# Attention with sigmoids and a token mixer on one core: the order of the work, three transposed head groups, double sigmoids and held loads

## The chip, the cores and the metric

The program runs on one core of a Trainium2 chip. Its engines are PE (TensorE, matrix products into PSUM), ACT (ScalarE), DVE (VectorE), POOL (GpSimd) and SP, which issues the DMAs. Each engine works through its own queue in order; semaphores make one wait for another. The metric is the device time of one execution in microseconds (us), as a median of several.

## The reference

For 8 batches and 12 heads, with sequences of 448 and head size 64, float32:

```python
scores = scale * np.matmul(q, k.transpose(0, 1, 3, 2)) - np.log(S)
attn = 1.0 / (1.0 + np.exp(-scores))
attn_out = np.matmul(attn, v)
x = attn_out.transpose(0, 2, 1, 3).reshape(B, S, H * D)
wq, wk = x @ w_q, x @ w_k
W_tok = scale * np.einsum('bsd,btd->bst', wq, wk)
mixed = np.einsum('bst,btd->bsd', W_tok, x)
out = np.maximum(mixed, 0.0) @ w_out
```

## The kernel before

Four heads of one batch make a group; there are 24 groups, three to a batch, counted from 0. Each group is cut into 7 tiles of 64 keys, so there are 168 tiles of scores, counted here from 1: tiles 1 to 7 belong to group 0, tile 8 is the first of group 1.

For each group q, k and v are loaded in float32 and cast to bf16, mostly by POOL. q and k are then transposed, in one of three ways, by the group's letter in the plan: on PE against an identity matrix and copied out of PSUM ("q", "k"); or by DVE in 32 x 32 blocks, from a layout that POOL has arranged ("c", "d") or in parts by DVE alone ("r", "s", "z"). On PE, `transposes` takes 28 products of 64 x 64 for one array, four of them side by side; `transposes_whole` takes 7 of 128 x 128 and has been used for group 0 alone. Groups 1 to 3 and 6 go by PE; of group 1 each array is copied out by itself (L280), of the others q and k together in one copy (L288).

`scores` makes one tile: four products of 64 x 448 into one pair of PSUM banks, and one sigmoid on ACT (L305) that writes an `at` tile, one of 16. `values` (L311) multiplies `at` with v and adds up over the seven tiles of a group; the result xt is copied out (L328) and transposed for the mixer (`tr_x`). When the three groups of a batch are done, the mixer follows: wq and wk (`mlp_wqk`), a transposition (`mlp_wkn`), `mlp_tmp`, `mlp_mix`, and the output projection in half-chunks of six or twelve products (`out_chunk`, `out_pair`), each copied out (L584, L530) and stored by SP.

PSUM is one array of eight banks, handed out as four pairs, 0 to 3, or as single banks a to h (a and b make pair 0, and so on to g and h in pair 3). Which one each step takes stands in the string BANKS.

The order is written out by hand: PLAN is a string of letters, and the loop at its end (L762) issues one step for each, onto the engines' queues. S makes a tile of scores, P a value product (its case says, where it is the last of a group, which engine copies out), q, k, c, d, r, s, z transpose, W, N, U, M are the mixer's steps, O and o half-chunks of the output with the copy by DVE or ACT, D lets one store be issued, E is four products of zeros whose result nobody uses, K the transposition of the last four parts of group 0's k, 1 a cast by DVE. Loads follow a list, ORDER, into a ring of six buffers (`pump_loads`, L658): a load is issued when the buffer's last content has been cast. Entries with a dot are cast by DVE.

The kernel has a mechanism by which a load waits for a matmul (`behind_product`, L174): places would be marked by "^" in ORDER and "G" in PLAN. Neither occurs, so no load waits in that way.

Of the kernel before, what the change touches and what calls it, by code (L numbers as in the profile page):

```python
# [10 lines left out]
BF16 = mybir.dt.bfloat16  # L11
U32 = mybir.dt.uint32
ACTF = mybir.ActivationFunctionType
# [4 lines left out]
def kernel(  # L18
# [12 lines left out]
    nc = tc.nc  # L31
    B, H, S, HD = q.shape
# [3 lines left out]
    P = 128  # L36
    NI, NP = 7, 64
# [18 lines left out]
    p_x = pool("x", 2)  # L56
    p_one = pool("one", 1)
    p_mx = pool("mx", 2)
# [4 lines left out]
    banks = ps_q.tile([P, 8, 512], F32, tag="banks", name="banks")  # L63
# [1 line left out]
    pairs = [banks[:, 2 * n : 2 * n + 2] for n in range(4)]  # L65
    pairs16 = [banks16[:, 2 * n : 2 * n + 2] for n in range(4)]
    BANKS = (
        "abcd01230100233111102130123012312123120c302302023d0231a30123"
        "01310321312302103210e13f01fe30123c20312032a32b3213023ab12313"
        "2b13231023a213023a2b13ab213a21302gh012g012012303e013210ef130"  # L70
        "fe1302302g102h120h120321gh201gh201g12302a123ba123013ab12312g"
        "h102312gh1023132132032013031201231231031a2102302132103103123"
        "13103213023a1203203102"
    )
    given = list("".join(BANKS))
    held = set()
# [41 lines left out]
    products = []  # L118
# [11 lines left out]
    def xt(u, j):  # L130
        return xts[u % 2 * NJ + j].rearrange("p i h n -> p h i n")


    TW = (2, 3,)


    PLAN = (
        "KSSESDDESD1SEDqEE1EDSSkpPppSDppPSSSqDS1kpSPDpSqSpSkSpPSPSxSx"
        "wrDSSDDSwwspSpPppSzPPSSrwSwWXSsPSPpSpPNPPSUSqSzMSSkSPPPDDSSp"
        "DMppDSPSxSDxMScSpPpPSSdPpSDPWwwSSWDrXwWSSOsONSPpPSppzpSPSOOS"  # L140
        "xSPrpPpSUpSPszPSOSOSoSoSppMSPPPPPSSwcWWOCwSSdxOwSMWSOSxOSDMp"
        "DPScpDppSPDPSOdDoSDpxPPSCPPrSDPPDSOOSNSsSOzoOOSUSXcSDPpdpSSP"
        "pPSPOOwSMSWoWwMSSOWWScCpPpSxpdpSpPSOOMrSPPpSPpSSPPOoNSSSDszo"
        "oDOoDpxDSPpDpxSppPDSuWcdwWSSMWOOSMSWwOOSDxppSPcPSpmpPDooDNSD"
        "SSdooooDSSxODOSUPSDpPDpDSpPDPOcDOSSSOoodOSpMPSppPSPPcSwWwoSM"
        "SdOwWSSWOONSPMpcpSPpSPPSdOoXSoSxoSOxSOpPSpcUPSppPSoOSdSxoOSP"
        "PPmppSPPoSoMcSoSOlmlLLSLLSdooDSODNyOpScpdppPSSPPOoSoSOSOOSUS"
        "oSOpSPpP1SPoSoPSPoSOxpPPmPpPpMllmllyllyooONoOUoommooMOOOOOOO"
        "ooooooOOooOo"
    )  # L150
    PLAN = "".join(PLAN)
    KIND = ["a"] + [t for t in PLAN if t in "qcr"]

    ld = {}
    SRC = dict(q=q, k=k, v=v)
# [70 lines left out]
    qk = {}  # L226
# [28 lines left out]
    def tr(n, nm, kind):  # L255
        t = "qk".index(nm)
        if kind == "s":
            return
        if kind == "r":
            qk[n] = p_qk.tile([P, 2, 2, NI, NP], BF16, tag="qk", name="qk")  # L260
            w = pq[n].rearrange("p e t i d y -> p e (t i d y)").bitcast(F32)
            for e in range(2):
                nc.vector.transpose(out=qk[n][:, e].rearrange("p t i n -> p (t i n)").bitcast(F32), in_=w[:, e])  # L263
            return
        if kind in "cd":
            assert n in arranged
            w = pq[n].rearrange("p e t i d y -> p e (t i d y)").bitcast(F32)[:, t]
            if t == 0:
                qk[n] = p_qk.tile([P, 2, 2, NI, NP], BF16, tag="qk", name="qk")
            nc.vector.transpose(out=qk[n][:, t].rearrange("p t i n -> p (t i n)").bitcast(F32), in_=w)  # L270
            return
        t16 = ld.pop((nm + "16", n))
        if t == 0:
            ps_qk[n] = bank2()
        fb, _, ps = ps_qk[n]
        transposes(ps[:, :, t * S : (t + 1) * S], t16, slice(0, NI))
        if n == 1:
            if t == 0:
                qk[n] = p_qk.tile([P, 2, 2, NI, NP], BF16, tag="qk", name="qk")
            nc.vector.tensor_copy(  # L280
                out=qk[n][:, :, t].rearrange("p h i n -> p h (i n)"), in_=ps[:, :, t * S : (t + 1) * S],
            )
# [12 lines left out]

    def scores(n, i):
        fb, sc, _ = bank2()
        for g in range(2):
            for h in range(2):
                mm(  # L300
                    sc[HALF[h], g, 0:S], qk[n][HALF[g], h, 1, i, :],
                    qk[n][HALF[g], h, 0].rearrange("p i n -> p (i n)"), start=True, stop=True,
                )
        at = p_at.tile([P, 2, S], BF16, tag="at", name="at")
        nc.scalar.activation(at, sc[:, :, 0:S], ACTF.Sigmoid, bias=attn_bias, scale=attn_scale)  # L305
        release(fb)
        ats[n, i] = at

    pv = {}

# [168 lines left out]
    chunks = []  # L479
    ot = {}  # L480

    opened = []
    stores, o_tiles = [], [0]
# [133 lines left out]
    def cols(r):  # L617
# [9 lines left out]
        out=ident, in_=ident, compare_op=ALU.not_equal, fill=1.0, base=0,  # L627
# [4 lines left out]
    for _ in range(32):  # L632
        mm(pairs[3][:, 0, 0:P], zeros[:, 0:P], zeros[:, 0:P], start=True, stop=True)


    ORDER = (
# [5 lines left out]
    )  # L642
    BY = {"s": [], "v": []}
    GATED = {(x.strip(".!^")[0], int(x.strip(".!^")[1:])) for x in ORDER.split() if "^" in x}
    gates = []
    for x in ORDER.replace("^", "").split():
# [5 lines left out]
    ORDER = [(x[0], int(x[1:])) for x in ORDER.replace(".", "").replace("!", "").replace("^", "").split()]  # L652
    done = dict.fromkeys("SPqkKxWNUMOCDz", 0)
    used, loaded, cast = set(), set(), set()

# [2 lines left out]
    def pump_loads():  # L658
        while len(loaded) < len(ORDER):
            nm, n = ORDER[len(loaded)]  # L660
            if len(ring) >= 6 and ring[-6] not in cast:
                break
            if (nm, n) in GATED and not gates:
                break
            m = gates.pop(0) if (nm, n) in GATED else 0
            ring.append((nm, n))
            if nm == "w":
                load_wout(n - 1, m) if n else load_weights()
            else:
                load1(n, nm, nc.sync, m)  # L670
            loaded.add((nm, n))
# [83 lines left out]
    used |= {("q", 0), ("k", 0)}  # L755
    pump()

    ALIKE = dict(c="q", r="q", j="k", d="k", s="k", X="x", y="x", Y="x", z="z", w="W", L="W", l="W")
    done["q"] = done["k"] = 1
    quads_r = []  # L760

    for t in PLAN:  # L762
# [9 lines left out]
        if t in "12":  # L772
            cast_one("vs"[int(t) - 1])
            continue
        if t == "G":
            gates.append(len(products) - 1)
            continue
# [61 lines left out]
    assert not chunks and not opened and not stores and not given and not any(BY.values())  # L839
# [1 line left out]
_INS = ['q', 'k', 'v', 'moe_w_q', 'moe_w_k', 'moe_w_out']  # L841
_OUTS = [((8, 448, 768), 'float32')]
# [25 lines left out]
```

## Time and profile before

| | us |
|---|---|
| median of 3 runs | 186.71 (186.39 to 190.08) |
| the profiled execution, whole | 187.86 |
| its span, first to last instruction | 186.0 |
| mean granted TensorE clock | 0.998 |
| HBM read, written | 35.78 MB, 11.01 MB |

A row of a group names the source line, the engine, the operation, what it writes and reads, the shapes and the count; then the time that the group was busy and the mean of one in ns; then the idle time before it and who ended it. A row of a timeline begins with its start and its length in us. Line L121 is the helper through which all products go, L124 the one for transpositions on PE, so that the tiles' names tell them apart. The end of a product is modelled; the distance of two starts is the safer reading.

### The profile page before, as it was taken

The numbers are of one execution on the slowest core, as the hardware profiler recorded it, in microseconds if no ns is written. First come the engines' busy times: TensorE is split into PE (matmuls) and PEld (weight loads), VectorE is DVE, ScalarE is ACT, GpSimd is POOL, SyncE is SP. The second block draws the span as 40 slices with busy tenths as digits, with TensorE's granted clock in tenths as the row PEclk, the third lists the DMA queues.
The fourth block names the chain that finished last, engine by engine and source line by source line (L and its number), as shares of the span: only waits on it lengthen the run. The fifth ranks groups of instructions, "written<-read, shape, count | busy, mean of one in ns | idle before, by whom it ended". The sixth has DMA issues, their size and how long they took to land.

```text
span 186.0 us, 8450 instructions
## 1 busy us (share of the span) xinstructions
PE 169.6 (91%) x3642; PEld 113.7 (61%) x3642; DVE 134.2 (72%) x206; ACT 158.7 (85%) x205; POOL 116.8 (63%) x156
## 2 busy tenths in 40 slices
PE   7697688789999999999997999999999999999980
PEld 7354435454664555655554556456788798879970
DVE  2545599979998998988985953589786875685430
ACT  4499999999999999999996899899989999966020
POOL 1236697998889996699949969798999300000000
PEclk9999999999999999999999999999999999999999
DMA  5998999979998799999999999995596243333665
GB/s 175 357 380 267 350 343 341 401 247 318 380 392 323 245 273 324 296 273 351 321 234 328 341 289 322 322 338 205 147 321 178 73 110 86 90 88 88 176 169 170
DMA packets 24309, 48.51 MB, mean 261 GB/s; under 512 B 3920, under 2 KB 16464, under 8 KB 24272
## 3 DMA queue, kind: packets, MB, share of 16 engines
q1 hardware_dynamic: 24112, 47.79, 79.6%
q8 instruction: 28, 0.46, 1.0%
q10 hardware_dynamic: 160, 0.20, 0.3%
q14 instruction: 9, 0.07, 0.1%
HBM read 35.78 MB, written 11.01 MB: 252 GB/s over the span
## 4 chain that ended last, share of the span: by engine, by line
PE 70%; DVE 12%; DMA 5%; ACT 4%; issue 3%; POOL 2%; SPq 0%; DVEq 0%; ACTq 0%; POOLq 0%
PE banks L121 67%; PE banks L124 4%; ACT at L305 4%; DVE qk L250 4%; DMA ld<-in_k_dram 2%; DMA ld<-in_moe_w_q_dram 2%; DVE xt L328 2%; DVE xn L357 2%; DVE qk L263 1%; DVE mx L442 1%; POOL wqk L693 1%; POOL qk L210 1%; DVE wqk L402 1%; DVE qk L288 1%; DVE k L220 0%
## 5 line engine op out<-in xcount | busy, mean ns | idle before, releaser
L305 ACT ACTIVATE at<-banks 128x896 bf16<-128x896 f32 x168 | 141.2, 937 | 7.7 <-PE banks L121 6.9
L121 PE MATMUL banks<-wout,mx 64*64 64x384 bf16 (+1 forms) x840 | 65.6, 324 | 0.3 <-issue 0.2
L121 PE MATMUL banks<-qk 64*64 64x448 bf16 x672 | 60.9, 358 | 5.2 <-ACT at L305 2.4
L210 POOL CAST qk<-ld 128x896 bf16<-128x896 f32 x38 | 44.6, 1190 | 9.7 <-issue 6.7
L121 PEld LDWEIGHTS <-mx 64*64 64x64 bf16 (+1 forms) x840 | 39.8, 105 | 16.4 <-issue 6.1
L121 PE MATMUL banks<-at,v 64*64 64x448 bf16 x672 | 47.5, 350 | 0.3 <-ACT at L305 0.2
L121 PEld LDWEIGHTS <-qk 64*64 64x64 bf16 x672 | 27.3, 105 | 25.6 <-issue 18.7
L328 DVE CAST xt<-banks 128x896 bf16<-128x896 f32 x23 | 24.9, 1084 | 9.4 <-PE banks L121 9.1
L121 PEld LDWEIGHTS <-v 64*64 64x64 bf16 x672 | 23.8, 106 | 5.8 <-issue 1.1
L442 DVE TENSOR_SCALAR mx<-banks 128x896 bf16<-128x896 f32 (+1 forms) x21 | 19.9, 955 | 3.9 <-PE banks L121 3.6
L220 POOL CAST v<-ld 128x896 bf16<-128x896 f32 x22 | 20.2, 929 | 2.2 <-DMA ld<-in_v_dram 1.7
L357 DVE COPY xn<-banks 128x896 bf16<-128x896 bf16 x20 | 12.5, 623 | 5.7 <-PE banks L124 4.9
L270 DVE STREAM_TRANSPOSE qk<-qk 128x448 f32<-128x448 f32 x26 | 16.0, 629 | 0.1
L250 DVE STREAM_TRANSPOSE qk<-qk 32x448 f32<-32x448 f32 x24 | 15.3, 636 | 0.6
L169 POOL COPY qk<-qk 32x448 uint32<-32x448 uint32 x26 | 14.4, 554 | 1.6
L172 POOL COPY qk<-swap 32x448 uint32<-32x448 uint32 x26 | 14.4, 554 | 1.5
L121 PE MATMUL banks<-xt,wqk 64*64 64x448 bf16 (+1 forms) x84 | 13.8, 353 | 0.3 <-ACT at L305 0.2
L124 PEld LDWEIGHTS <-xt 64*64 64x64 bf16 (+1 forms) x588 | 9.9, 108 | 2.3 <-DVE xt L328 0.4
L584 DVE COPY o<-banks 128x384 f32<-128x384 f32 x17 | 9.4, 551 | 2.2 <-PE banks L121 1.5
L124 PE MATMUL banks<-ident,xt 64*64 64x64 bf16 (+1 forms) x588 | 10.4, 194 | 0.1
L121 PE MATMUL banks<-wqk,tmp 64*64 64x224 bf16 (+1 forms) x72 | 8.8, 290 | 0.1
L121 PE MATMUL banks<-wq,tmp 64*64 64x224 bf16 (+1 forms) x72 | 8.5, 292 | 0.0
(67 smaller groups left out, 135.6 us busy)
## 6 DMA issues: line engine op xcount, KB each, us to landing
ld<-in_q_dram SPq DMA_DIRECT2D x24, 448.0 KB, 6.3
ld<-in_v_dram SPq DMA_DIRECT2D x24, 448.0 KB, 6.1
ld<-in_k_dram SPq DMA_DIRECT2D x23, 448.0 KB, 6.0
out_dram<-o SPq DMA_DIRECT2D x38, 192.0 KB, 4.4
ld<-in_moe_w_out_dram SPq DMA_DIRECT2D x6, 384.0 KB, 4.9
out_dram<-ld SPq DMA_DIRECT2D x12, 192.0 KB, 2.8
wout<-wout SPq DMA_DIRECT2D x6, 192.0 KB, 7.6
out_dram<-ld SPq DMA_DIRECT2D x6, 96.0 KB, 3.2
```

The lines of the kernel that those rows point to most:

```text
L121: products.append(nc.tensor.matmul(*args, **kw))
L124: products.append(nc.tensor.transpose(*args, **kw))
L169: eng.tensor_copy(out=w[lo, 1], in_=w[hi, 0])
L172: eng.tensor_copy(out=w[hi, 0], in_=z[lo])
L210: COPY[e](out=f[:, :, "qk".index(nm)].rearrange("p e i d y -> p e y i d"), in_=ld.pop((nm, n)).rearrange("p (y i e d) -> p e y i d", y=2, ...
L220: COPY[e](out=t16.rearrange("p i b d -> p b i d"), in_=ld.pop((nm, n)).rearrange("p b (i d) -> p b i d", i=NI),)
L250: nc.vector.transpose(out=qk[n][other : other + 32, h].rearrange("p t i n -> p (t i n)").bitcast(F32), in_=w[own : own + 32, 1 - h],)
L270: nc.vector.transpose(out=qk[n][:, t].rearrange("p t i n -> p (t i n)").bitcast(F32), in_=w)
L305: nc.scalar.activation(at, sc[:, :, 0:S], ACTF.Sigmoid, bias=attn_bias, scale=attn_scale)
L328: COPY[eng](out=xt(u, j), in_=ps)
L357: COPY[eng](out=xn, in_=ps)
L442: nc.vector.tensor_scalar(dst, ps, moe_scale, 0.0, ALU.mult, ALU.max)
```

## The change

Four things change, and the written-out order is a new one.

1. Groups 1, 2 and 3 are transposed by `transposes_whole`: 7 products of 128 x 128 for q and 7 for k, each array into a single bank and copied out by DVE by itself (letters a, b). Group 6 alone is still transposed by 28 products.
2. A step T makes the scores of a tile without a sigmoid; the next S makes another tile, and then one sigmoid covers both, reading two bank pairs in one access with a step between them. The 16 `at` tiles become one array, so that two neighbours can be written at once. T occurs four times: tiles 2 and 3, 6 and 7, 116 and 117, 124 and 125 share a sigmoid.
3. A table BEHIND names 18 loads and, for each, a matmul by its number, behind which the load begins. The older marks are gone.
4. PLAN, BANKS and ORDER are new. There are ten E instead of six; two more xt tiles are transposed whole (Y); the first tile of scores stands ahead of K; w_q and w_k are loaded ahead of group 3 and cast by DVE; D occurs 77 times, not 46.

```diff
-    p_at = pool("at", 16)
+    at_all = singles.tile([P, 16, 2, S], BF16, name="at")
...
-        "KSSESDDESD1SEDqEE1EDSSkpPppSDppPSSSqDS1kpSPDpSqSpSkSpPSPSxSx"
+        "SDKTSDDSEEEESTEES1abEESD1PpPSpppDPSDaSbSDEDPS1PSDPSDPxSESPDD"
...
-        "DPScpDppSPDPSOdDoSDpxPPSCPPrSDPPDSOOSNSsSOzoOOSUSXcSDPpdpSSP"
+        "pPNDDppPPSDSODDOOcSTSOOOoSdxSoXDpDcSdPDDppSPUpDSPSDDOoDTSODD"
...
-    KIND = ["a"] + [t for t in PLAN if t in "qcr"]
+    KIND = ["a"] + [t for t in PLAN if t in "qacr"]
...
         t16 = ld.pop((nm + "16", n))
+        if kind in "ab":
+            fb, _, ps = bank1()
+            transposes_whole(ps, t16, slice(0, NI))
+            if t == 0:
+                qk[n] = p_qk.tile([P, 2, 2, NI, NP], BF16, tag="qk", name="qk")
+            nc.vector.tensor_copy(
+                out=qk[n][:, :, t].rearrange("p h i n -> p i h n"),
+                in_=ps[:, 0 : NI * P].rearrange("p (i h n) -> p i h n", h=2, n=NP),
+            )
+            release(fb)
+            return
...
-    def scores(n, i):
+    begun = []
+
+    def scores(n, i, alone):
...
-        at = p_at.tile([P, 2, S], BF16, tag="at", name="at")
-        nc.scalar.activation(at, sc[:, :, 0:S], ACTF.Sigmoid, bias=attn_bias, scale=attn_scale)
-        release(fb)
-        ats[n, i] = at
+        begun.append((fb, n, i))
+        if not alone:
+            return
+        slot = (NI * begun[0][1] + begun[0][2]) % 16
+        begun.sort()
+        for x, (_, m, c) in enumerate(begun):
+            ats[m, c] = at_all[:, slot + x]
+        if len(begun) == 1:
+            dst, src = at_all[:, slot], sc[:, :, 0:S]
+        else:
+            (lo, _, _), (hi, _, _) = begun
+            dst = at_all[:, slot : slot + 2]
+            src = banks.rearrange("p (a b) x -> p a b x", b=2)[:, lo : hi + 1 : hi - lo, :, 0:S]
+        nc.scalar.activation(dst, src, ACTF.Sigmoid, bias=attn_bias, scale=attn_scale)
+        for f, _, _ in begun:
+            release(f)
+        begun.clear()
...
+    BEHIND = {('v', 3): 216, ('q', 5): 216, ('k', 5): 216, ('k', 6): 216, ('q', 7): 216, ('w', 4): 216, ('v', 5): 472, ('w', 6): 472, ('k', 9): 600, ('q', 11): 856, ('v', 11): 984, ('k', 13): 1112, ('v', 14): 1368, ('v', 16): 1496, ('q', 17): 1496, ('k', 20): 1880, ('v', 22): 2264, ('v', 23): 2392}
...
-            if (nm, n) in GATED and not gates:
+            m = BEHIND.get((nm, n), 0)
+            if m >= len(products):
                 break
-            m = gates.pop(0) if (nm, n) in GATED else 0
...
-        if t == "S":
-            scores(*divmod(c, NI))
+        if kind == "S":
+            scores(*divmod(c, NI), t == "S")
```

What this does to the queues shows in the built programs, row by row in their order. First ACT, from its last copy for group 0 on; `at` are the sigmoids' results. Before:

```order
L740 COPY qk_164<-banks_85 128x3x2x64
L305 ACTIVATE at_206<-banks_85 128x896
L305 ACTIVATE at_212<-banks_85 128x896
L305 ACTIVATE at_222<-banks_85 128x896
L305 ACTIVATE at_232<-banks_85 128x896
L305 ACTIVATE at_244<-banks_85 128x896
```

And now:

```order
L765 COPY qk_162<-banks_82 128x3x2x64
L330 ACTIVATE at_89<-banks_82 128x896
L330 ACTIVATE at_89<-banks_82 128x1792
L330 ACTIVATE at_89<-banks_82 128x896 x2
L330 ACTIVATE at_89<-banks_82 128x1792
L330 ACTIVATE at_89<-banks_82 128x896 x51
L461 CAST tmp_1248<-banks_82 128x384
```

Seven sigmoids have become five, two of them over two tiles, and a copy for the mixer has come in after the 58th tile.

Next PE, at the last scores of group 0 that stand ahead of group 1's transposition (q16_234 before, q16_180 now, is q of group 1; qk_164, qk_162 group 0's transposed q and k; the brackets name the engines waited for). Before:

```order
L121 LDWEIGHTS qk_164
L121 MATMUL banks_85<-qk_164 64x448 [waits Activation_49]
L121 LDWEIGHTS zeros_91
L121 MATMUL banks_85<-zeros_91 64x448 [waits Activation_49]
L124 LDWEIGHTS q16_234 [waits DVE_49]
L124 MATMUL banks_85<-ident16_90,q16_234 64x64
```

And now:

```order
L121 LDWEIGHTS zeros_88
L121 MATMUL banks_82<-zeros_88 64x448
L121 LDWEIGHTS qk_162
L121 MATMUL banks_82<-qk_162 64x448
L124 LDWEIGHTS q16_180 [waits Pool_49]
L124 MATMUL banks_82<-ident16_87,q16_180 128x128 [waits Activation_49]
```

The transposition now stands behind all seven tiles of group 0, not behind some of them, and its first product waits for ACT; the count that it waits for is the one that the second sigmoid over two tiles brings.

Last PE at the scores of tiles 115 to 117 (qk) and the output projection behind them (wout, mx). Before:

```order
L121 MATMUL banks_85<-qk_2542 64x448 [waits Activation_49]
L121 LDWEIGHTS qk_2542
L121 MATMUL banks_85<-qk_2542 64x448
L121 LDWEIGHTS mx_2113
L121 MATMUL banks_85<-wout16_86,mx_2113 128x384 [waits Activation_49]
```

And now:

```order
L121 MATMUL banks_82<-qk_2262 64x448 [waits Activation_49]
L121 LDWEIGHTS qk_2262
L121 MATMUL banks_82<-qk_2262 64x448
L121 LDWEIGHTS mx_1913
L121 MATMUL banks_82<-wout16_83,mx_1913 128x384 [waits Activation_49]
```

The rows read alike. The count behind the last bracket was that of an earlier copy by ACT; it is now that of the sigmoid over tiles 116 and 117, whose scores stand directly ahead.

More of the change, by code (lines that the diff above doesn't have):

```diff
@@ L67 @@
     BANKS = (
[L68 to L73, printed above, removed]
+        "abcd012301222220333cd222103e0f1330210200c21a2310e3101013f013"
+        "2a103103120312030231203123c2032d0c3d20c32320312031e31f301232"
+        "cd30230c230230132c302131ef301efg01203120c230dc230230121g2013"
+        "2a32ba312b3210323ab21321b321a30cd230cd203c203103c02dc302130c"
+        "d3202dc302130cd320131231201201321321021301301201303c21320120"
+        "320310312312012g12a3201203102"
     )
@@ L131, in xt @@
         return xts[u % 2 * NJ + j].rearrange("p i h n -> p h i n")
-    TW = (2, 3,)
+    TW = (2, 3)
     PLAN = (
-        "KSSESDDESD1SEDqEE1EDSSkpPppSDppPSSSqDS1kpSPDpSqSpSkSpPSPSxSx"
-        "wrDSSDDSwwspSpPppSzPPSSrwSwWXSsPSPpSpPNPPSUSqSzMSSkSPPPDDSSp"
-        "DMppDSPSxSDxMScSpPpPSSdPpSDPWwwSSWDrXwWSSOsONSPpPSppzpSPSOOS"
-        "xSPrpPpSUpSPszPSOSOSoSoSppMSPPPPPSSwcWWOCwSSdxOwSMWSOSxOSDMp"
-        "DPScpDppSPDPSOdDoSDpxPPSCPPrSDPPDSOOSNSsSOzoOOSUSXcSDPpdpSSP"
[L143 to L149, printed above, removed]
+        "SDKTSDDSEEEESTEES1abEESD1PpPSpppDPSDaSbSDEDPS1PSDPSDPxSESPDD"
+        "aDSDDpPSbSxSDSwWPrPSPSPspSzPDPwSSDWSrwXWSsSSpDPPNSpPSDzpUSPS"
+        "MSqkSSpPPppSxPSPMSSxSpcPPSMpPSDpPSWDwWSWDdSSwSrDWXSoOSOSsPNS"
+        "pPppSzpPSOCSDxSuSPrCpSppSPsPzooSPSoOSpcPMSppSPpPSOdWwxSDSOwW"
+        "xcSOSMSWwOMSpdPpSPPPDPSDSOOSPDPpSxDpPSPDPSOONSScSdoOXoSOSDDU"
+        "DSPPpSpSpcPCPSdoOSMSwoWSMDSDWwWwOSSPPpcxPpSpdPSOODSMrDpDppsD"
+        "SPPSpOoDSSPDDNzDOoSSxooDUScDpPPSxPPPSPSwwOSMwDoWdSMSowoWSpmp"
+        "pDNDDppPPSDSODDOOcSTSOOOoSdxSoXDpDcSdPDDppSPUpDSPSDDOoDTSODD"
+        "ooOSMPppSpcDppSPSWdOwDMSWwwoSDDSWooNSMPPDSPpppSDcdSPYOOSSoxO"
+        "cSoxSOpSpppSUSppPSOSodxSOSPOSPPpSPcDPPSOmoMSOmOlSdLlllLSoSOO"
+        "DSxpocDpSNppSppPS1oOSOSdDOOSoSSOopDpUPSPPpSPOSDOSoSoPpyPppmp"
+        "PlLMLDLMYLloOxoNOoUoODMomoMOOooOOooOoOOOooOOoO"
     )
     PLAN = "".join(PLAN)
-    KIND = ["a"] + [t for t in PLAN if t in "qcr"]
+    KIND = ["a"] + [t for t in PLAN if t in "qacr"]
     ld = {}
@@ L651 @@
     OTHERS = set(BY["s"] + BY["v"])
-    ORDER = [(x[0], int(x[1:])) for x in ORDER.replace(".", "").replace("!", "").replace("^", "").split()]
+    ORDER = [(x[0], int(x[1:])) for x in ORDER.replace(".", "").replace("!", "").split()]
     done = dict.fromkeys("SPqkKxWNUMOCDz", 0)
@@ L774 @@
             continue
-        if t == "G":
-            gates.append(len(products) - 1)
-            continue
         kind = ALIKE.get(t, t if t in "qkx" else t.upper())
@@ L838 @@
                 out_chunk(t == "o", tail)
-    assert not chunks and not opened and not stores and not given and not any(BY.values())
+    assert not begun and not chunks and not opened and not stores and not given and not any(BY.values())
 _INS = ['q', 'k', 'v', 'moe_w_q', 'moe_w_k', 'moe_w_out']
```

6 lines of the change are left out of this document (2 added, 4 removed), and 10 rows, old and new, of the table ORDER.

## The prediction

> **What bounds the kernel now.** I read the page's head first, then its chain of waits, the busiest group, and the timeline of ACT by itself.
>
> ```profile
> span 186.0 us, 8450 instructions
> PE 169.6 (91%) x3642; PEld 113.7 (61%) x3642; DVE 134.2 (72%) x206; ACT 158.7 (85%) x205; POOL 116.8 (63%) x156
> PE 70%; DVE 12%; DMA 5%; ACT 4%; issue 3%; POOL 2%; SPq 0%; DVEq 0%; ACTq 0%; POOLq 0%
> L305 ACT ACTIVATE at<-banks 128x896 bf16<-128x896 f32 x168 | 141.2, 937 | 7.7 <-PE banks L121 6.9
> ```
>
> PE and ACT are both nearly full, and 70% of the chain is PE. The shares hide two regimes, which ACT's own timeline shows:
>
> ```profile
> 5.12 0.48 ACT L740 COPY qk<-banks 128x384 bf16<-128x384 bf16 x1 [0.57 <-PE banks L124]
> 7.46 13.16 ACT L305 ACTIVATE at<-banks 128x896 bf16<-128x896 f32 x16 [1.86 <-PE banks L121]
> 20.80 39.03 ACT L305 ACTIVATE at<-banks 128x896 bf16<-128x896 f32 x47 [0.18 <-PE banks L121]
> 59.73 0.47 ACT L584 COPY o<-banks 128x384 f32<-128x384 f32 x1
> ```
>
> From 7.46 to 59.8 us ACT runs 63 sigmoids with one gap of 0.18 us. Sixteen take 13.16 us, the last of them 0.94, so one starts every (13.16 - 0.94) / 15 = 0.815 us. This stretch is bound by ACT: whatever delays a sigmoid there delays all later ones, and PE has too little other work to make it up. Later PE leads:
>
> ```profile
> 20.00:30.00 10.00, 8.09 (x160) 4.27 (x160) 8.92 (x13) 9.82 (x13) 8.92 (x11) 1.00 0.99 353
> 110.00:120.00 10.00, 10.00 (x160) 5.62 (x153) 5.32 (x9) 9.16 (x14) 7.86 (x11) 1.00 0.93 318
> PE banks L121 <- ACT at L305: 3.5, 12, 0.5
> PE banks L121 <- DVE xn L357: 1.4, 1, 1.4
> ```
>
> In the rows by windows (PE, PEld, DVE, ACT, POOL busy), PE is busy 8.09 of 10 us early and 10.00 later, with ACT at 9.16: neither can absorb a long wait of the other. PE waited for sigmoids only 3.5 us in all, at most 0.5 at once, and 1.4 once for an xn copy.
>
> **The opening, part by part.** These are its rows:
>
> ```profile
> 4.52 0.56 PE L124 MATMUL banks<-ident,q 128*128 128x128 bf16 x7
> 5.13 0.63 PE L124 MATMUL banks<-ident,k 128*128 128x128 bf16 x3
> 6.71 0.51 PE L124 MATMUL banks<-ident,k 64*64 64x64 bf16 x16 [0.95 <-DVE k L750]
> 7.05 0.55 PE L121 MATMUL banks<-qk 64*64 64x448 bf16 x8
> 7.09 0.49 DVE L736 COPY qk<-banks 128x256 bf16<-128x256 bf16 x2 [0.44 <-PE banks L124]
> 7.44 0.38 PE L121 MATMUL banks<-zeros 64*64 64x448 bf16 x4
> 7.63 0.38 PE L121 MATMUL banks<-qk 64*64 64x448 bf16 x4
> 9.28 0.93 POOL L220 CAST k<-ld 128x896 bf16<-128x896 f32 x1 [2.37 <-DMA ld<-in_k_dram]
> 9.97 0.62 DVE L280 COPY qk<-banks 128x896 bf16<-128x896 bf16 x1 [1.29 <-PE banks L124]
> 17.09 0.93 POOL L220 CAST k<-ld 128x896 bf16<-128x896 f32 x1 [0.21 <-DMA ld<-in_k_dram]
> L440 ACT ACTIVATE mx<-banks 128x448 bf16<-128x448 f32 x6 | 3.1, 550 | 1.5 <-PE banks L121 1.4
> L440 ACT ACTIVATE mx<-banks 128x896 bf16<-128x896 f32 x3 | 2.8, 929 | 0.0
> ```
>
> *First tile.* Now the first scores stand ahead of the products of K, which wait until 6.71 for a load. They can begin when the third whole k product ends (5.13 + 0.63 = 5.76). From scores to sigmoid took 7.46 - 7.05 = 0.41, so the first sigmoid starts at 6.17, not 7.46.
>
> *First sigmoid over two tiles* (tiles 2 and 3). No such row exists. By the two L440 rows 448 more elements cost 929 - 550 = 379 ns, so 896 more make 937 + 758 = 1.69 us; two starts apart (1.63) and two whole ones (1.87) bound it. Sigmoids overlap by 0.937 - 0.815 = 0.12, so the next could start 1.57 after it, not 1.63: 0.06 gained, 0.2 for four, which I leave out as less than the rest is uncertain by. The Trainium skill's ScalarE: Activation LUTs, section What ACT_TABLE_LOAD costs, has back-to-back ACTIVATEs overlapping by about 93 ns beside a fixed 186; by it four would gain 0.4. Its tiles' scores start after K at 7.05 and 7.24, so it runs from 7.65 (the L736 copies end at 7.58) to 9.34. It reads bank pairs 3 and 0 in one stepped access, and in the built program every later product in a bank lying between them waits for its end. Tile 4 uses pair 1: its scores start at 9.39, its sigmoid at 9.80. By the old cadence the fourth was at 7.46 + 3 x 0.815 = 9.91, so the early start is already spent.
>
> *Second sigmoid over two tiles* (tiles 6 and 7). Four products take 7.63 - 7.44 = 0.19 us. After tile 4 come four dummies (0.76), tiles 5 and 6, two dummies and tile 7, whose scores start at 9.39 + 0.19 + 0.76 + 0.38 + 0.38 = 11.10. The sigmoid could start at 11.51; ACT, with tile 5 from 10.75, is free at 11.57. It ends at 13.26. Again it spans all four pairs, and next on PE stand group 1's whole-array transposes in bank 2, which wait for it. Behind them in PE's queue stand two dummies and tile 8, the next food of ACT. So: transposes from 13.31, read out 0.56 later at 13.87, two copies of 0.62 on DVE (q, then k) to 15.11, tile 8's scores, and its sigmoid at 15.56. Before, the eighth sigmoid came at 7.46 + 7 x 0.815 = 13.17. **Opening: +2.4 us**; at least 0 if that wait covered nothing (group 1's later load, k, had landed by 9.28), at most +2.8 with 1.87 for each double.
>
> *Whole-array transposes.* Six arrays now go in 7 products.
>
> ```profile
> 46.60 0.41 PE banks L124 x7
> 63.85 0.22 PE banks L124 x28
> 88.77 1.15 PE L121 MATMUL banks<-wout,mx 128*128 128x384 bf16 x6
> 89.85 0.38 PE L121 MATMUL banks<-wqk,tmp 64*64 64x448 bf16 x2
> 94.37 2.11 PE L121 MATMUL banks<-wout,mx 128*128 128x384 bf16 x12
> 96.41 0.38 PE L121 MATMUL banks<-at,v 64*64 64x448 bf16 x4
> ```
>
> The same transposition of an xt tile took 0.41 us of the chain in 7 products and 0.22 in 28: fewer products are slower by 0.19, or 1.1 for six. Changing between 64 and 128 rows costs too: six products held PE 89.85 - 88.77 = 1.08 us and twelve 96.41 - 94.37 = 2.04, so six are 0.96 and 0.12 is left for leaving the mode; entering is taken to cost the same. All this falls before 25 us, where PE waits for ACT anyway, and the part in tile 8's path is in the +2.4. Two xt tiles more go whole as well, late, where PE leads: 2 x 0.19, and one pair of mode changes more there, 0.24 (the order has 46 entries into 128 rows, not 39, six of them for q and k): **+0.6**. The Trainium skill's TensorEngine Tiling (Array Packing), section Key Properties, says that changing the tiling mode drains the TensorE; it gives no price, and the 0.12 agrees with it. The Trainium skill's TensorE: Matmul & The Clock Gate, Part 4, gives a whole-array transpose about 275 ns in a kernel, which would make 42 of them 11.6 us; the 0.41 for seven here contradicts that, and the measurement decides.
>
> *Other moves of the opening.* The cast of w_q, w_k goes from POOL to DVE and its load ahead of group 3's; group 3 is needed 14 sigmoids after tile 8, at 15.56 + 14 x 0.815 = 27 us, and its k had landed by 17.09 before, so I book 0. One more copy stands on ACT before its 64th sigmoid:
>
> ```profile
> L435 ACT CAST tmp<-banks 128x384 bf16<-128x384 f32 x1 | 0.5, 474 | 0.0
> ```
>
> That is **+0.4**; DVE loses the same copy, and is not the bound.
>
> *Held loads.* All sit in SP's queue, so later loads and the stores behind them wait too.
>
> ```profile
> ld<-in_v_dram SPq DMA_DIRECT2D x24, 448.0 KB, 6.1
> POOL v L220 <- DMA ld<-in_v_dram: 1.7, 3, 1.2
> L220 POOL CAST v<-ld 128x896 bf16<-128x896 f32 x22 | 20.2, 929 | 2.2 <-DMA ld<-in_v_dram 1.7
> ```
>
> By the built order the loads held to product 472 are let go at tile 33, and v of group 5 is first read after tile 43: ten sigmoids, 8.2 us, against 6.1 to land and 0.93 to cast. The others have as much or more. I take 0; the margin of 1.1 us, if a landing were twice as long, would become 5 us of PE standing at the first value product, so the bounds are 0 and +5.
>
> **The late sigmoids over two tiles** (tiles 116 and 117, 124 and 125) fall where PE leads. Each time the next product on PE is one of the output projection, in bank 3, between the pairs that the sigmoid spans, and it waits for the sigmoid's end; on PE all else is queued behind it. First place: tiles 115 to 117 start 0.19 apart. If t is the start of the first, its sigmoid starts at t + 0.41, the double one at t + 1.23 and ends at t + 2.92; PE was free at t + 0.57. Stall 2.4 us. Then come four half-chunks without scores, so ACT idles. Second place: no scores directly ahead, so the double starts at t + 0.60 and ends at t + 2.29, against t + 0.38: 1.9 us. **Late: +4.3**; nothing, if PE would have stood there for another reason.
>
> **The sum.** 2.4 + 0.6 + 0.4 + 4.3 = +7.7 at most of the likely. The rest of the order is new too. Before, PE waited 4.9 us for sigmoids and the xn copy (the two rows above); some of these waits will be swallowed by the new ones, since DVE and ACT catch up while PE stands. I take off 2.2, not quite half: **+5.5**. The profiled execution took 187.86 us around its span of 186.0; the median of the runs shown is 186.71. On the profiled execution that is 193.4, on the median **192.2**.
>
> **Rivals.** *Only the opening counts* (20%): the late waits fall where PE has to stand anyway. For it: ACT is 9.16 of 10 busy there; against it: PE's longest wait for a sigmoid was 0.5. Then 186.71 + 2.4 + 0.6 + 0.4 - 1.0 = 189.1, within 2%. *The new order wins* (5%): ACT starts at 6.17 and keeps 1.3 us, and in PE's stretch the 4.9 us of waits vanish: 186.71 - 1.3 - 4.9 = 180.5. The point at which this decides is tile 8: if its sigmoid starts by 12 us, the double ones hold nothing back. For it speaks that two tiles' own banks are free sooner; against it the waits in the built program. The Trainium skill's PSUM — Partial Sum Buffer, section PSUM bank collisions raise a hardware error, asks for guards by bank and quadrant, so by it the banks between would need no wait; no row of before shows one. *A held load comes late* (5%): v of group 5 stands 4 us longer: 196. *The change does nothing* on balance (3%): 186.7. The forecast has 67%; alone it reaches from 190 to 194.4 (+7.7).
>
> About 2%, 183.0 to 190.4, is what a measurement of this kernel can tell from no change. Slower: 65% of the forecast's 67 and the held load, 70%. Faster: 5%. Within: 25%. The range of 8 in 10 takes in the opening alone and most of the full sum with its unknown costs: 188.6 to 195.5.
>
> **What would show it.** ACT's timeline: first sigmoid near 6.2, a gap of about 2.3 us after the seventh tile, tile 8 near 15.6, then no gap to the 63rd; the waits of PE: about 2 us twice for a sigmoid near 115 to 130 us; the two-tile row near 1.69 us. The forecast is wrong if tile 8 comes by 13.2, or if PE's waits for sigmoids stay near 3.5 us in all.

## The result: 198.44 us, slower by more than forecast

The changed kernel took 198.44 us (median of 4 runs, 197.98 to 199.06), the kernel before 187.43 beside it (median of 4, 186.39 to 190.08). The ratio is 1.057, 95% interval 1.051 to 1.062; here and below a ratio leaves out executions that took over 1.5% longer than the fastest of the same kernel, while the medians hold all. The profiled execution took 199.06 us, 11.2 more than that of before. Slower was forecast, but 192.2 us, with a range up to 195.5, was too little.

The head of the page after, with the granted clock in 40 slices (about 4.9 us each) and the shares of the chain:

```profile
span 197.3 us, 8139 instructions
PE 176.3 (89%) x3490; PEld 114.4 (58%) x3490; DVE 132.5 (67%) x203; ACT 163.0 (83%) x205; POOL 119.5 (61%) x157
PEclk9856999999999999999999999999999999999998
PE 71%; DVE 15%; ACT 6%; DMA 2%; issue 2%; SPq 0%; ACTq 0%; DVEq 0%
```

PE has 152 products fewer and is busy 6.7 us longer. The clock row (tenths of full speed) has a 5 and a 6 in the third and fourth slices, where PE was granted about half of its clock. ACT's own timeline after shows the opening:

```profile
6.38 0.92 ACT L330 ACTIVATE at<-banks 128x896 bf16<-128x896 f32 x1 [0.48 <-PE banks L121]
7.78 1.66 ACT L330 ACTIVATE at<-banks 128x1792 bf16<-128x1792 f32 x1 [0.48 <-PE banks L121]
10.13 0.92 ACT L330 ACTIVATE at<-banks 128x896 bf16<-128x896 f32 x1 [0.68 <-PE banks L121]
12.00 0.92 ACT L330 ACTIVATE at<-banks 128x896 bf16<-128x896 f32 x1 [0.95 <-PE banks L121]
13.49 1.66 ACT L330 ACTIVATE at<-banks 128x1792 bf16<-128x1792 f32 x1 [0.58 <-PE banks L121]
18.21 0.92 ACT L330 ACTIVATE at<-banks 128x896 bf16<-128x896 f32 x1 [3.06 <-PE banks L121]
```

The shape is the forecast one: an early first sigmoid (6.17 worked out, 6.38 measured), then two over two tiles, each followed by a hole. But tile 8 comes at 18.21 us, not at 15.56. PE's rows of the same stretch:

```profile
9.50 0.59 PE L121 MATMUL banks<-qk 64*64 64x448 bf16 x4 [1.76 <-ACT at L330]
9.82 1.75 PE L121 MATMUL banks<-zeros 64*64 64x448 bf16 x16
15.21 0.91 PE L124 MATMUL banks<-ident,q 128*128 128x128 bf16 x7 [1.76 <-ACT at L330]
```

And rows by windows (the length; PE, PEld, DVE, ACT, POOL busy; the granted clock; DMA share and GB/s):

```profile
7.00:9.00 2.00, 0.73 (x16) 0.27 (x17) 0.55 (x2) 1.52 (x2) 0.45 (x1) 0.88 1.01 378
9.00:11.00 2.00, 1.50 (x20) 0.92 (x21) 0.63 (x1) 1.32 (x2) 0.56 (x2) 0.50 1.05 392
13.00:15.00 2.00, 0.44 (x8) 0.10 (x1) 0.00 (x0) 1.51 (x1) 1.24 (x2) 0.50 1.08 275
17.00:19.00 2.00, 2.00 (x28) 0.78 (x24) 1.68 (x2) 0.79 (x1) 1.54 (x2) 0.56 0.08 31
```

PE stood 1.76 us behind each double sigmoid, as worked out (free at 7.24 + 0.38, the next product at 9.39: 1.77). What was not worked out is the clock: it was 0.50 from 8.50 us, within the first stand, to 18.74 us (the 0.88 and 0.56 above are means of windows that are only in part within that time). So sixteen dummies took 1.75 us where 0.76 had been booked, and the seven products of q 0.91. PE's longest waits in all:

```profile
PE banks L121 <- ACT at L330: 8.1, 12, 2.2
PE banks L124 <- ACT at L330: 2.0, 2, 1.8
PE banks L121 <- DVE xn L383: 2.2, 2, 2.0
```

The two stands of the late part, in PE's timeline, and the group of the double sigmoids:

```profile
119.58 2.11 PE L121 MATMUL banks<-wout,mx 128*128 128x384 bf16 x12 [2.25 <-ACT at L330]
129.67 2.11 PE L121 MATMUL banks<-wout,mx 128*128 128x384 bf16 x12 [1.82 <-ACT at L330]
```

```profile
L330 ACT ACTIVATE at<-banks 128x1792 bf16<-128x1792 f32 x4 | 6.6, 1662 | 1.1 <-PE banks L121 1.1
```

Of the 10.1 us for which PE waited for sigmoids (3.5 before), four stands make 7.6: 1.76 twice, 2.25 and 1.82. The last two had been worked out as 2.4 and 1.9, the length of a double sigmoid, 1662 ns, as 1.69 us. New is a wait of 2.0 us for an xn copy. Its rows:

```profile
22.11 2.39 POOL L210 CAST qk<-ld 128x896 bf16<-128x896 f32 x2 [2.65 <-DMA ld<-in_k_dram]
22.15 4.00 DVE L718 CAST wqk<-ld 64x384 bf16<-64x384 f32 x4
26.18 0.63 DVE L383 COPY xn<-banks 128x896 bf16<-128x896 bf16 x1
26.86 0.38 PE L121 MATMUL banks<-zeros 64*64 64x448 bf16 x4 [2.00 <-DVE xn L383]
27.48 6.07 ACT L330 ACTIVATE at<-banks 128x896 bf16<-128x896 f32 x7 [1.44 <-PE banks L121]
```

The four casts of w_q and w_k, moved to DVE, took 4.00 us from the first start to the last end (2.2 on POOL before); the xn copy queued behind them, PE stood for it, and ACT lost 1.44 us. The starts of five sigmoids, read from ACT's rows one by one, divide the loss (us; two tiles under one sigmoid are counted as two):

| tile | before | after | later by |
|---|---|---|---|
| 8 | 13.06 | 18.21 | 5.15 |
| 22 | 24.88 | 31.82 | 6.94 |
| 113 | 107.53 | 114.98 | 7.45 |
| 127 | 122.11 | 133.10 | 10.99 |
| 162 | 156.01 | 166.81 | 10.80 |

So about 7 us are lost before tile 22 (2.4 had been forecast), 0.5 over the next ninety tiles, 3.5 around the two late double sigmoids, and none later. Three explanations had to be told apart: the products in the banks *between* the two pairs wait for the double sigmoid, and the clock falls while PE stands; or a double sigmoid costs by itself, wherever its banks lie; or the new order and the whole-array transposes cost, and the double sigmoids little.

### The profile page after: what moved, and what is told of

Its sections match the earlier page's. It is cut to its first block, busy times and chain, and to the rows that moved or that the text cites. A ratio compares the mean times of both kernels' runs of the same rounds, so it can differ in the third digit from the quotient of the medians.

```text
span 197.3 us, 8139 instructions
## 1 busy us (share of the span) xinstructions
PE 176.3 (89%) x3490; PEld 114.4 (58%) x3490; DVE 132.5 (67%) x203; ACT 163.0 (83%) x205; POOL 119.5 (61%) x157
## 4 chain that ended last, share of the span: by engine, by line
PE 71%; DVE 15%; ACT 6%; DMA 2%; issue 2%; SPq 0%; ACTq 0%; DVEq 0%
PE banks L121 66%; ACT at L330 5%; PE banks L124 5%; DVE qk L250 4%; DMA ld<-in_k_dram 2%; DVE xt L354 2%; DVE mx L468 2%; DVE wqk L718 2%; DVE qk L278 1%; DVE qk L263 1%; DVE xn L383 1%; DVE wqk L428 1%; DVE wkn L448 0%; DVE wqk L413 0%; DVE o L610 0%
## 5 line engine op out<-in xcount | busy, mean ns | idle before, releaser
L330 ACT ACTIVATE at<-banks 128x896 bf16<-128x896 f32 (+1 forms) x164 | 142.0, 946 | 14.5 <-PE banks L121 13.1
L121 PE MATMUL banks<-wout,mx 64*64 64x384 bf16 (+1 forms) x840 | 66.4, 323 | 4.3 <-ACT at L330 4.3
L121 PEld LDWEIGHTS <-qk 64*64 64x64 bf16 x672 | 26.0, 106 | 25.9 <-issue 18.5
L121 PEld LDWEIGHTS <-v 64*64 64x64 bf16 x672 | 22.4, 107 | 7.3 <-issue 2.0
L220 POOL CAST v<-ld 128x896 bf16<-128x896 f32 x23 | 21.5, 939 | 8.3 <-DMA ld<-in_v_dram 6.6
L270 DVE STREAM_TRANSPOSE qk<-qk 128x448 f32<-128x448 f32 x28 | 17.5, 632 | 0.1
L169 POOL COPY qk<-qk 32x448 uint32<-32x448 uint32 x28 | 15.6, 556 | 1.7
L172 POOL COPY qk<-swap 32x448 uint32<-32x448 uint32 x28 | 15.6, 556 | 1.6
L250 DVE STREAM_TRANSPOSE qk<-qk 32x448 f32<-32x448 f32 x20 | 12.7, 636 | 0.5
L121 PE MATMUL banks<-zeros 64*64 64x448 bf16 (+1 forms) x72 | 8.1, 434 | 3.0 <-DVE xn L383 2.0
```

The lines of the kernel that those rows point to most:

```text
L121: products.append(nc.tensor.matmul(*args, **kw))
L169: eng.tensor_copy(out=w[lo, 1], in_=w[hi, 0])
L172: eng.tensor_copy(out=w[hi, 0], in_=z[lo])
L220: COPY[e](out=t16.rearrange("p i b d -> p b i d"), in_=ld.pop((nm, n)).rearrange("p b (i d) -> p b i d", i=NI),)
L250: nc.vector.transpose(out=qk[n][other : other + 32, h].rearrange("p t i n -> p (t i n)").bitcast(F32), in_=w[own : own + 32, 1 - h],)
L330: nc.scalar.activation(dst, src, ACTF.Sigmoid, bias=attn_bias, scale=attn_scale)
```

## The experiments

Twelve kernels ran, all of them the changed kernel with one to three parts altered, except the last. Ratios are against the kernel before in the same batch, whose median was 187.9 to 188.4 us; 0.01 is 1.9 us.

**The same double sigmoids on neighbouring pairs.** Only the names in BANKS are permuted (pair 0 becomes 1, 1 becomes 3, 3 becomes 0), so that every double sigmoid reads two adjacent pairs and no bank lies between. The first row of the table:

```diff
-        "abcd012301222220333cd222103e0f1330210200c21a2310e3101013f013"
+        "cdgh132013222221000gh222310e1f3001231211g23c2031e0313130f130"
```

> The bank pairs are renamed throughout (0 to 1, 1 to 3, 2 to 2, 3 to 0); plan, loads and all four sigmoids over two tiles stay. Each of these sigmoids now reads two neighbouring pairs, so that no bank lies between them. Theory A (the loss is the wait of products in the banks between, with the lower TensorE clock that the standing brings): tile 8's sigmoid starts between 12.6 and 13.6 us, not 18.2; the granted clock from 10 to 20 us is 1.0; PE's waits for sigmoids fall from 10.1 us to under 4.5; 188 to 191 us. Theory B (a sigmoid over two tiles is harmful in itself, since two pairs come free only at its end): over 195 us, and the waits stay. Theory C (the new order and the whole-array transposes cost the time): over 196 us, with the waits gone.

188.96 us, ratio 1.006 (1.000 to 1.012). Its windows, and the row of its waits for sigmoids:

```profile
10.00:20.00 10.00, 8.39 (x164) 4.86 (x164) 6.94 (x11) 9.92 (x12) 5.43 (x6) 1.00 1.07 349
120.00:130.00 10.00, 10.00 (x158) 5.73 (x159) 7.13 (x11) 9.39 (x13) 9.45 (x14) 1.00 0.98 362
```

```profile
PE banks L121 <- ACT at L330: 2.9, 10, 0.6
```

Same order, same instructions, same number of double sigmoids; the long waits are gone (0.6 us at most), the clock is full, tile 8 comes at 13.16 us. Some 9.5 us of the 10.6 that the ratio 1.057 stands for go with a renaming of banks. That a double sigmoid costs by itself, or that the order does, falls with this run, but for the 0.006 that is left.

**No double sigmoid.** The four letters T become S, in the two rows of PLAN that hold them:

```diff
-        "SDKTSDDSEEEESTEES1abEESD1PpPSpppDPSDaSbSDEDPS1PSDPSDPxSESPDD"
+        "SDKSSDDSEEEESSEES1abEESD1PpPSpppDPSDaSbSDEDPS1PSDPSDPxSESPDD"
...
-        "pDNDDppPPSDSODDOOcSTSOOOoSdxSoXDpDcSdPDDppSPUpDSPSDDOoDTSODD"
+        "pDNDDppPPSDSODDOOcSSSOOOoSdxSoXDpDcSdPDDppSPUpDSPSDDOoDSSODD"
```

> Each of the four T of the plan becomes S, so every tile has its own sigmoid again; all else stays as changed. Theory A: as with neighbouring pairs, within 1 us of that run: 188 to 191 us, tile 8 by 13.6 us. Theory B: 188 to 191 us as well, but 4 us or more below the run with neighbouring pairs. Theory C: over 196 us.

188.73 us, ratio 1.005 (1.000 to 1.009), no different from the neighbouring pairs: a double sigmoid is worth nothing measurable here, once it holds nobody up.

**Without the two early ones** (only the first of these two rows), and **without the two late ones** (only the second):

> Only the two early sigmoids over two tiles (2 and 3, 6 and 7) are split into single ones. Theories A and B: the opening's loss goes, tile 8 by 13.6 us and clock 1.0 from 10 to 20 us, the two late waits of about 2 us stay: 192.5 to 194.5 us. Theory C: over 196 us.

> Only the two late sigmoids over two tiles (116 and 117, 124 and 125) are split. Theories A and B: tile 8 stays at 18.2 us, the gaps of ACT near 117 to 133 us go: 194 to 195.5 us. Theory C: over 196.5 us. If the early and the late gain add up to that of all four, the two are independent.

Without the early: 192.25 us, ratio 1.020 (1.013 to 1.026), just under the range expected. Without the late: 195.31 us, ratio 1.038 (1.033 to 1.044). The early two are thus worth 1.057 - 1.020 = 0.037, 7.0 us, the late two 0.019, 3.5 us, each to within about 1.6; together 10.5, against 9.8 for all four at once. They add up. Each profile keeps the waits that the other loses. PE's waits for sigmoids without the early ones (tile 8 at 13.51 us):

```profile
PE banks L121 <- ACT at L330: 6.3, 11, 2.2
```

And without the late ones (tile 8 at 17.76):

```profile
PE banks L121 <- ACT at L330: 4.2, 10, 1.8
```

**The waits kept, the clock kept up.** Two pairs are renamed (2 and 3), so that 22 dummy steps E, in place of 8, may stand in free banks ahead of the waiting products. The double sigmoids and the waits behind them stay; in the opening PE works while it would stand. Tiles 4 and 5 come to stand side by side, with their dummies ahead of them. The first row of PLAN:

```diff
-        "SDKTSDDSEEEESTEES1abEESD1PpPSpppDPSDaSbSDEDPS1PSDPSDPxSESPDD"
+        "SDKTSDDEEEEEEEESSTEEEEEESEEEEEEEE1abEESD1PpPSpppDPSDaSbSDEDP"
```

> As changed, with its four sigmoids over two tiles, but the bank pairs 2 and 3 are renamed into each other, so that the two early ones leave one pair free, and dummy products of zeros stand in that pair while PE waits for them: 22 in the opening instead of 8. The waits stay, PE is busy in them. Clock theory (PE standing lowers the granted clock, and that costs as much as the waits themselves): granted clock 1.0 from 10 to 20 us instead of 0.56, tile 8 between 15.3 and 16.4 us as worked out at full clock, 195 to 196.8 us in all. Rival (the waits alone delay tile 8 to 18.2 us): tile 8 at 17.5 us or later, 197.5 us or more.

196.10 us, ratio 1.044 (1.036 to 1.053). Two windows of it, and ACT's row of tile 8:

```profile
7.00:9.00 2.00, 2.00 (x48) 1.28 (x52) 0.55 (x2) 1.52 (x2) 0.79 (x2) 1.00 1.04 391
13.00:15.00 2.00, 2.00 (x38) 1.16 (x30) 0.69 (x2) 0.58 (x1) 1.39 (x2) 1.00 1.18 278
```

```profile
15.96 4.24 ACT L331 ACTIVATE at<-banks 128x896 bf16<-128x896 f32 x5 [2.37 <-PE banks L121]
```

With the clock kept up, tile 8 comes at 15.96 us, against 15.56 by hand and 18.21 in the changed kernel, and the rival falls. The wait alone is 15.96 - 13.06 = 2.9 us, the lowered clock 2.25 more at tile 8.

In time the difference is 1.057 - 1.044 = 0.012, 2.3 us, with intervals that just overlap, and it is not the price of the clock alone. In this profile the casts of w_q and w_k were short as well (1.71 us, not 4.00), and PE waited 0.2 us for xn, not 2.0. At tile 113 it is therefore 4.2 us ahead of the changed kernel. But 1.7 of that is lost again behind the third double sigmoid, where nothing fills the stand:

```profile
115.41 3.79 PE L121 MATMUL banks<-wout,mx 128*128 128x384 bf16 x12 [2.25 <-ACT at L331]
115.66:119.05 3.39, 3.39 (x12) 1.36 (x10) 1.33 (x3) 0.00 (x0) 0.00 (x0) 0.50 0.51 199
```

The same twelve products after the same stand of 2.25 us took 2.11 us in the changed kernel, at a granted clock of 1.00.

**The cast of w_q and w_k on POOL again**, all else as changed (the first rows of ORDER and PLAN; without its third 1 the row of PLAN takes in the next letter):

```diff
-        "q1 .k1 v0 .k2 q2 v1 .w0 q3 k3 k4 q4 v2 v3 q5 k5 v4 w1 q6 k6 k7 "
+        "q1 .k1 v0 .k2 q2 v1 w0 q3 k3 k4 q4 v2 v3 q5 k5 v4 w1 q6 k6 k7 "
...
-        "SDKTSDDSEEEESTEES1abEESD1PpPSpppDPSDaSbSDEDPS1PSDPSDPxSESPDD"
+        "SDKTSDDSEEEESTEES1abEESD1PpPSpppDPSDaSbSDEDPSPSDPSDPxSESPDDa"
```

> The changed kernel with all four double sigmoids; only the second load of w_q and w_k is cast on POOL again, as before the change. Theory D (the cast on VectorE, 4.0 us there in the changed kernel's profile, holds back the copy of xn for which TensorE stood 2.0 us): the step between the starts of the sigmoids of tiles 15 and 22, 7.5 us in the changed kernel's profile, falls to 6.0 to 6.3, and the time is 0.8 to 1.8 us under the changed kernel's, 196.6 to 197.8. Theory E (the place of the cast costs nothing, the long stretch there is what is left of the lowered clock): step 7 or more, 198 to 199.

197.83 us, ratio 1.052 (1.046 to 1.058). In the profile the step from tile 15 to tile 22 falls from 7.52 us to 5.58, and PE's wait for xn from 2.0 to 0.2, even below the 6.0 to 6.3 of theory D. The time lies between the ranges of the two theories: 0.0046, 0.9 us, less than the changed kernel, with intervals that overlap. And it moves with the clock: three of the six executions had a mean granted clock of 0.988 to 0.990 and took 196.0 to 197.1 us, three had 0.962 to 0.965 and took 198.6 to 199.1; the four of the changed kernel had 0.971 to 0.983. So the place of the wait is shown, and its price in time is not told apart from nothing.

**No double sigmoid, and the cast on POOL** (both edits above):

> No sigmoid over two tiles, and the four casts of w_q and w_k go to POOL again instead of DVE, their load standing where the change put it. If those casts on DVE cost something by themselves: 186 to 187.8 us, tile 22 by 24.6 us in the profile, and runs closer together than 187.5 to 192.3 us. If they are slow only where the early waits have shifted them: within 0.6 us of the run without double sigmoids (188.7).

187.82 us, ratio 1.001 (0.997 to 1.005), 0.9 us under the run with the casts on DVE, with overlapping intervals and between the two ranges expected; tile 22 at 25.08 us, not by 24.6. With the double sigmoids and the casts undone, the rest of the change (order, whole-array transposes, held loads) leaves the time where it was. The doubles are worth 1.052 - 1.001 = 0.051, 9.6 us, between these two kernels.

**28 products for groups 1 to 3**, q and k in one bank pair as before the change (in BANKS the single banks make way for pairs); first with the cast on DVE, then on POOL, no double sigmoid in either:

```diff
-        "SDKSSDDSEEEESSEES1abEESD1PpPSpppDPSDaSbSDEDPS1PSDPSDPxSESPDD"
-        "aDSDDpPSbSxSDSwWPrPSPSPspSzPDPwSSDWSrwXWSsSSpDPPNSpPSDzpUSPS"
+        "SDKSSDDSEEEESSEES1qkEESD1PpPSpppDPSDqSkSDEDPS1PSDPSDPxSESPDD"
+        "qDSDDpPSkSxSDSwWPrPSPSPspSzPDPwSSDWSrwXWSsSSpDPPNSpPSDzpUSPS"
```

> No sigmoid over two tiles, and groups 1 to 3 are transposed in 28 products again instead of 7, q and k of a group into one bank pair held until both are there (groups 2 and 3 with one copy for both). The prediction's reading is that the 1.1 us which 7 products cost more is covered by ACT: within 0.7 us of the run without double sigmoids (188.7). If it is not covered: 187.3 us or less. If the single bank and the separate copies help: 189.7 us or more.

> No double sigmoid, w_q and w_k cast on POOL, and q and k of groups 1 to 3 transposed in 28 products again, not 7 whole-array ones, with one copy for q and k. To be read beside the same kernel with 7 products, 187.82 us. If the whole-array form is worth what the two kernels with the cast on VectorE differed by (1.5 us): 189 to 190.2. If that was the cast's varying length: 187.3 to 188.6. If the 7 products cost time, as the added changes of the array's mode in the prediction would have it (0.2 us and two copies more): 187.2 to 187.6.

190.20 us, ratio 1.011 (1.004 to 1.019), and 190.25 us, ratio 1.012 (1.007 to 1.017). On POOL the interval lies just clear of the 1.001 (0.997 to 1.005) with seven products, so in this order the seven-product form saves about 1.1%, 2.1 us; I had booked the early ones at nothing, inside the wait for tile 8. PE's rows of the second kernel show where:

```profile
13.19 0.41 PE L124 MATMUL banks<-ident,k 64*64 64x64 bf16 x28 [0.85 <-DVE qk L291]
23.11 0.41 PE L124 MATMUL banks<-ident,q 64*64 64x64 bf16 x28 [1.26 <-ACT at L330]
```

The products are no slower, but with q and k in one pair group 1's k waits for the copy of q, and group 3's q for a pair that a sigmoid still reads. What helps is the single bank, then, as far as these two rows tell; product form and banks were not changed apart.

**No load held**, again with the cast on DVE and on POOL, no double sigmoid:

```diff
-    BEHIND = {('v', 3): 216, ('q', 5): 216, ('k', 5): 216, ('k', 6): 216, ('q', 7): 216, ('w', 4): 216, ('v', 5): 472, ('w', 6): 472, ('k', 9): 600, ('q', 11): 856, ('v', 11): 984, ('k', 13): 1112, ('v', 14): 1368, ('v', 16): 1496, ('q', 17): 1496, ('k', 20): 1880, ('v', 22): 2264, ('v', 23): 2392}
+    BEHIND = {}
```

> No sigmoid over two tiles, and no load is held behind a matmul. The prediction booked the holds at 0: within 0.7 us of the run without double sigmoids (188.7). If they cost time: 187.7 us or less; if they help by keeping urgent loads ahead: 189.7 us or more.

> No double sigmoid, w_q and w_k cast on POOL, and none of the 18 loads held, so that each is issued as soon as its buffer is free. To be read beside the same kernel with the loads held, 187.82 us. Theory F (the holds are worth about 1%: without them the second half has a gap near tiles 141 to 148, and loads take POOL's and the queues' time too early): 189.3 to 191. Theory G (the 2.2 us between the two kernels with the cast on VectorE were the run-to-run length of that cast, not the holds): 187.3 to 188.8.

190.89 us, ratio 1.016 (1.007 to 1.025), and 188.93 us, ratio 1.005 (1.002 to 1.009). The second lies between the ranges of F and G. Its interval overlaps that with the holds, so that 0.9 us for the holds is not told apart from nothing. The first profile was longer by 4 us at its last tiles. Of these, 2.2 came between tiles 15 and 22, where its casts on DVE took 790 ns each against 543 with the holds and the granted clock was 0.50 from 20.97 to 24.38 us, and 1.6 between tiles 141 and 148, the gap of theory F; in the second profile that gap was 0.4. Whether the holds gain a little stays open; no run shows that they cost anything.

**The kernel before, with the first tile of scores ahead of K**, the part of the change by which the first sigmoid starts earlier:

```diff
-        "abcd01230100233111102130123012312123120c302302023d0231a30123"
+        "abcd20130100233111102130123012312123120c302302023d0231a30123"
...
-        "KSSESDDESD1SEDqEE1EDSSkpPppSDppPSSSqDS1kpSPDpSqSpSkSpPSPSxSx"
+        "SKSESDDESD1SEDqEE1EDSSkpPppSDppPSSSqDS1kpSPDpSqSpSkSpPSPSxSx"
```

> [...] If ScalarE's train of sigmoids sets the opening: first sigmoid 6.3 to 6.5, ratio 0.994 to 0.997 (186.9 to 187.4 beside 188.0). If the second tile's scores come no earlier, since TensorE or K's transposes set them: tile 8 at 13.0 to 13.1 as before, ratio 0.999 to 1.002.

187.57 us, ratio 0.999 (0.995 to 1.003). In its profile the first sigmoid starts at 6.80 us (7.46 before, 6.38 in the changed kernel) and tile 8 at 12.40, 0.66 earlier than before; in time nothing is told apart, and neither the 6.3 to 6.5 expected of the first sigmoid nor the 13.0 to 13.1 of tile 8 came true. No kernel of the study is shown to beat the one before.

## Why the prediction was right in kind and wrong in size

*The mechanism stood.* The forecast was a product in a bank between the two pairs, waiting for the double sigmoid. All four waits occurred at their places with nearly their lengths, and with adjacent pairs they go, and the loss with them. The page of the Trainium skill cited there (PSUM — Partial Sum Buffer, section PSUM bank collisions raise a hardware error) would have needed no wait for those banks; the built program waits all the same, 1.76, 1.76, 2.25 and 1.82 us.

*The opening, +2.4, was mis-sized: 5.15 us at tile 8, 6 to 7 in the runs.* The wait itself held: at full clock it put tile 8 at 15.96 us, 0.4 from the 15.56 worked out, and cost 2.9. The step that failed was to take the products behind the wait at their full-clock durations from before (the four products of a dummy step 0.19 us, the seven of a transposition 0.56). From within the first stand on the granted clock was 0.50 and not 1.00, and tile 8 came 2.25 us later than with the stands filled; 1.65 and 1.80 in the two other traces that have both stands unfilled (tile 8 at 17.61 and 17.76). So the size of this step differs between executions, which the last section shows. The trace of before had no such stand in the opening, so its rows held no price for it. The Trainium skill's TensorE: Matmul & The Clock Gate, section What's actually happening, has the clock halved after an idle window of about 3.4 us and given back after as much sustained work; the 0.50 agrees with the half, while here the clock fell during a stand of 1.76 us, after 3.39 us in which PE had been busy 1.98.

*The cast on DVE was booked at 0* because group 3 was not needed before 27 us. I looked at who needs the cast's result, and not at what is queued behind the cast on DVE: the xn copy, for which PE stood 2.0 us. It cost 1.9 us in the profile; in time, 0.9 is not told apart from nothing.

*The late waits, +4.3, were nearly right:* 3.5 both between tiles 113 and 127 and by the run without them. The waits themselves were 2.25 + 1.82 = 4.1; about half a microsecond was swallowed.

*The 2.2 taken off for waits swallowed elsewhere were not found.* Outside the four stands PE still waited 10.1 - 7.6 = 2.5 us for sigmoids and 2.2 for xn copies, 4.7 in all, where it had been 4.9. Together with +0.6 and +0.4 the term made -1.2; without double sigmoids and with the casts on POOL the rest came to +0.1 (-0.6 to +0.9). The full sum, +7.7 or 194.4 us, was nearer; the range went only a little past it, and no term of it held a lowered clock.

*The whole-array transposes* of q and k were booked as slower products whose cost ACT covers. With 28 products instead, the time was 2.1 us higher: the change of banks that goes with them had no price in the prediction. Its remark that 0.41 us for seven contradicts 275 ns for one was a misreading: in the rows of before one such product lasts 219 to 226 ns on average, and seven take 0.41 to 0.56 us because they overlap. No term used it.

*The sum as measured*, in ratios of 188 us: double sigmoids 9.6 (early about 6 to 7, of which the lowered clock is 2.25 at tile 8; late 3.5), casts on DVE 0.9, all the rest 0.1: 10.6. They are differences of ratios taken one after the other, so they add up by themselves; the 0.9 and the 0.1 are not clear of noise.

*The rivals.* That only the opening counts fell with the late 3.5 us; that the new order wins fell at its own point of decision, tile 8 at 18.21 instead of 12; that a held load comes late fell with the runs without holds, which are no faster.

## What to carry to other kernels

In these programs an access that strides over banks also holds up products in the banks it steps over, so choose neighbours for it: one renaming of banks was worth 5%. When a change makes TensorE stand in an opening that has little slack, price the products behind the stand at half the clock, the lowest granted in these traces, as an upper end. And when a step moves to another engine, ask first what is queued behind it there; who needs its result comes second.

## What the runs showed of the hardware that was not expected

*After some stands PE gets half its clock, in steps of 3.41 us.* In all fourteen traces the granted clock is either 1.00 or 0.50, and it changes only at distances of 3.41 us or multiples of it, on a grid that lies elsewhere in each execution. Four steps of the run without the two late double sigmoids:

```profile
6.69:10.09 3.40, 1.38 (x32) 0.70 (x36) 0.88 (x4) 2.57 (x2) 1.35 (x2) 1.00 1.03 390
10.11:13.50 3.39, 3.38 (x40) 1.83 (x32) 0.43 (x1) 1.83 (x2) 0.93 (x1) 0.50 1.11 345
13.52:16.91 3.39, 1.44 (x22) 0.91 (x22) 1.00 (x2) 1.66 (x1) 1.87 (x2) 1.00 0.94 273
16.93:20.33 3.40, 3.21 (x36) 1.63 (x40) 0.67 (x2) 1.83 (x2) 1.87 (x2) 0.50 0.55 166
```

Here each step in which PE was busy 1.38 or 1.44 us is followed by one at half the clock. The changed kernel and the one with the casts on POOL have the same products on PE up to 16 us, and both stood 1.76 us twice. The first had 0.50 for three steps, from 8.50 to 18.74 us, the second for one, from 9.80 to 13.22. The window from 13 to 15 us of the changed kernel stands above; that of the other:

```profile
13.00:15.00 2.00, 0.54 (x8) 0.10 (x1) 0.00 (x0) 1.61 (x2) 1.72 (x2) 0.95 1.21 276
```

Tile 8 came at 18.21 and 17.61 us. What a stand costs is thus in part luck. Not every stand has this price: the late ones of 2.25 and 1.82 us left the clock of the changed kernel at 1.00, while the same 2.25 us in the run with the filled waits were followed by one step at 0.50. And a double sigmoid is not needed for it: in two kernels without any (casts on POOL, with seven and with 28 products) PE stood 1.11 and 1.64 us ahead of K and had 0.50 for one step, from 7.16 and 7.81 us on. The Trainium skill's page named above (TensorE: Matmul & The Clock Gate) calls the gate's window free-running; a grid that lies elsewhere in each execution agrees. From what share of busy time on the clock stays up, these runs do not show.

*The same cast on DVE takes 0.4 us or over 1.4.* The four casts of w_q and w_k (64 x 384), with the shortest, the median and the longest in ns and the starts of the first and the last, in the changed kernel:

```profile
L718 DVE CAST wqk<-ld x4: 420/1052/1437, 22.2 to 25.2; 64x384 bf16<-64x384 f32 x4
```

And in the one with the filled waits:

```profile
L719 DVE CAST wqk<-ld x4: 404/420/422, 19.5 to 20.8; 64x384 bf16<-64x384 f32 x4
```

In the first, POOL casts from 22.11 to 24.50 us and again from 24.80; in the second POOL has no cast between 19.23 and 21.34. Across the runs the four took 1.7 to 4.0 us. The Trainium skill's SBUF — State Buffer, section Who interferes with whom, gives the two engines a port pair that one instruction holds to its end, in a mode that casts among others can enter; the longest cast here exceeds the shortest by 1.02 us, less than one cast of POOL beside it (2.39 / 2 = 1.2), which agrees. So does this: the three long casts ended at 23.59, 24.78 and 26.15 us, each 0.27 or 0.28 after a cast of POOL had ended.
